# GpSimd's table units of the last stage in one go: from four gated places to slot 34

## The chip, the cores and the metric

The kernel runs on one core of one Trainium2 chip. A core has five engines with a queue of instructions each: TensorE (PE: matrix products; its weight loads are listed as PEld), VectorE (DVE), ScalarE (ACT), GpSimd (POOL) and SyncE (SP), and 16 DMA engines that they share. Each engine works through its own queue in order and waits on semaphores for the others. The metric is the time of one execution on the device in microseconds, as the median of several runs. The profile is one more execution, recorded by the hardware profiler; its times count from the first instruction. "L410" is line 410 of the kernel's file.

## The reference

Eight sequences of 3008 tokens with 256 channels are filtered by a Fourier transform along the sequence, a product with a complex filter and the transform back. Each token then goes through a feed-forward layer of 2048 hidden units with an exact GELU:

```python
X = np.fft.rfft(x, axis=1)
y = np.fft.irfft(X * (filt_r + 1j * filt_i)[None], n=x.shape[1], axis=1)
h = y.reshape(24064, 256) @ w_in
g = 0.5 * h * (1.0 + erf(h / sqrt(2)))
out = g @ w_out
```

## The kernel before, in words

**Stages.** The transform of length 3008 = 47 x 64 is done by matrix products with tables of sines and cosines. Batch 0 has a path of its own at the start (`c1` to `c4`). For each of the batches 1 to 7 there are four stages: `fold` and `s1` (over the 47), `s2` (over the 64) with the filter, `s3` (back over the 64) and `s4` (back over the 47). Between the stages the data are turned by writing them to DRAM and reading them back on SP's queue (`R1`, read by `r1` into `b_sb`; `R2`, read by `r2` into `d_sb`). `s4` writes its result into a ring `y_sb` of two batches.

**The feed-forward layer** goes over tiles of 512 tokens, 47 of them. `mm1` makes one of 16 blocks of hidden units: two products into a `ps_h` bank of PSUM (there are three), and GELU by ACT (L643) into `g_sb`. The second product follows a tile later. For tiles 0 to 2 it is plain (`mm2_first`; VectorE copies the result to `ost` at L660). From tile 3 on, `mm2_seven` does it in seven half-size products m = 0 to 6 in the manner of Strassen and Winograd. VectorE makes their sums of inputs (`sums_1` L685, `sums_2` L691, `sums_3` L696) and puts the results together (L729 to L743) from two `ps_o` banks: m = 0 goes to one, m = 1 and 2 to the other, m = 3 and 4 to the first again, m = 5 and 6 to the second again. The product m = 2 reads what L691 makes, m = 6 what L696 makes. `ost`, `t_sb` and the two results of a tile share a pool of four output buffers. Most output rows are stored by DMAs that GpSimd issues (L761), a few by SP.

**Order of the work.** It is written by hand: the program's main loop has 16 slots per tile, each with one `mm1` and a sixteenth of the second product, and `put(slot, function, arguments)` hangs everything else on a slot; what hangs on a slot is issued before the slot's products. Each engine gets its instructions in the order in which the loop issues them. In the trace slot 27 begins at 58.6 us, slot 33 at 63.4, slot 49 at 78.7 and slot 64 at 93.6; a slot lasts 0.75 to 0.87 us. For batch 1, `s2` stands at slots 27, 41 and 54, `s3` at 38, 52 and 66. `s2_out` (L467) multiplies the result of `s2`, in PSUM, with the filter `Fu`, in SBUF; `s2_sum` (L473, L474) adds and subtracts halves of these products; `s3` needs these sums, first those of one part, in its second half those of the other.

**The filter.** It is loaded into a tile `F` and moved by 36 DMAs of SP into the order `Fu` (`move_filters`, L130; the last 20 at slot 18). The space of `F` is then used again: one piece for `s4_sb`, the sums that L696 makes, two for `v_sb`, and one, `T4a`, for the table of `s4`.

**The table of `s4`.** `table_4_rows` and `weights_4` (slot 9, GpSimd) prepare rows and weights. `table_4_factors` turns them by three small products (L391) and three evacuations by ACT into the factors `G` and `fcs`. `table_4_all` makes the table out of the factors in eight units, each for eight of 32 columns and one of two halves: two products (L410) into a scratch tile `tmp_sb` and their sum (L412) into `T4a`. The scratch tile comes from the pool of `d_sb`, of three buffers. The first `s4` of batch 1 runs on TensorE at 107.4 us. In the kernel before, the factors stand at slot 49, and the units go by twos, at slots 67, 87, 98 and 105, each call with a scratch tile of its own. Ahead of those at 67, 87 and 98 stands a gate: `gate` copies one element of a tile on GpSimd, so that GpSimd's queue waits there until the tile is written.

**GpSimd's queue** also issues the loads of x for the next batch (`load_next`: a gate, then L101), at slots 32, 34, 42, 46, 76, 77, 80 and 81 for batch 2, and the output stores of L761. `fold` (L109, L110) needs these loads.

Of the kernel before, what the change touches and what calls it, by code (L numbers as in the profile page):

```python
# [20 lines left out]
HB = 32  # L21
# [761 lines left out]
def kernel(  # L783
# [9 lines left out]
    m = _Mix(ctx, tc, x, filt_r, filt_i, moe_w_in, moe_w_out, out)  # L793
# [4 lines left out]
    g = m.small  # L798
# [113 lines left out]
    def put(slot, f, *a):  # L912
        at.setdefault(slot, []).append((f, a))
# [5 lines left out]
    for b in range(1, B):  # L919
# [5 lines left out]
        for c in range(4):  # L925
            slot = (4, 8, 11, 13)[c] if b == 1 else s1 + int(c * n1)
# [46 lines left out]
    put(9, m.table_4_rows, g)  # L973
    put(9, m.weights_4, g)
    put(23, m.table_u)
    put(49, m.table_4_factors, g)
    for t, slot in ((3, 67), (5, 98)):
        put(slot, lambda t=t: m.gate(m.st["s", t][0:1, 7, 1, 255:256]))
    put(87, lambda: m.gate(m.st["x1"][0:1, 1, 11, 0:1]))
    parts = [(w, h) for w in range(0, HB, 8) for h in range(2)]  # L980
    for i, slot in enumerate((67, 87, 98, 105)):
        put(slot, m.table_4_all, parts[2 * i:2 * i + 2])
    put(18, m.move_filters, 2, 4)
    put(20, m.weight_sums)
    plain = (0, 1, 2)
# [9 lines left out]
    for s in range((NT + 1) * 16):  # L995
        t, jc = s // 16, s % 16
# [44 lines left out]
```

## Time and profile before

| what | us |
|---|---|
| median of 3 runs (733.98 to 734.56) | 734.04 |
| span of the profiled execution, first to last instruction | 732.0 |
| TensorE busy, share of the span | 713.6, 97% |
| VectorE busy | 597.0, 82% |
| ScalarE busy | 576.5, 79% |
| GpSimd busy | 286.2, 39% |

The profiled execution's own time is its span of 732.0 us and what lies around it; the runs' median is 2.0 us more than the span. The TensorE clock was granted in full (0.999). The page gives each engine's busy time, and for each wait what ended it; a wait of an engine that is not the bound costs nothing by itself. In a timeline the columns are the start, the time (with several instructions in one row: from the first start to the last end), engine, line, operation, what is written from what, shapes and the number of instructions; in brackets stands the idle time ahead and what ended it. In the list of waits the columns after the colon are the sum, the number of waits and the longest.

GpSimd's time around the table:

| stretch, us | GpSimd |
|---|---|
| 63.8 to 67.8 | gates and x loads of slots 32 and 34 |
| 70.9 to 79.1 | stores, gates and x loads of slots 42 and 46 |
| 87.4 to 96.3 | two groups of three stores |
| 96.4 to 103.4 | table units 1 and 2 |
| 104.3 to 115.1 | gates, x loads of slots 76 to 81, stores |
| 115.3 to 120.7 | table units 3 and 4 |
| 127.8 to 140.8 | table units 5 to 8 |

### The profile page before, as it was taken

The page shows a single profiled execution, that of the slowest core. Times are in us where ns is not written, and L with a number is a line of the kernel's source. Part 1 is how long each engine was busy: PE and PEld are TensorE (multiplying, and loading weights), DVE is VectorE, ACT ScalarE, POOL GpSimd, SP SyncE. Part 2 cuts the span into 40 slices and gives each one's busy share as a digit, 9 for nine tenths or more (in the row PEclk, how much of TensorE's full clock was granted, in tenths as well). Part 3 has the DMA queues.
Part 4 walks back from the last instruction along what each step waited for, and adds up shares of the span by engine and source line. Part 5 has one row for each costly group of instructions (what it writes and reads, how often), then busy time and mean ns, then how long its engine had stood idle before and what let it go on. Part 6 is the DMA issues. An engine that isn't in the chain of part 4 may idle for free.

```text
span 732.0 us, 22073 instructions
## 1 busy us (share of the span) xinstructions
PE 713.6 (97%) x9016; PEld 505.9 (69%) x9165; DVE 597.0 (82%) x1091; ACT 576.5 (79%) x1050; POOL 286.2 (39%) x546
## 2 busy tenths in 40 slices
PE   7999999999999999999999999999999999999997
PEld 4846675676777666666677667666677767777776
DVE  8975698899878998798976999779988897775666
ACT  7997778688877888778887788877888788877773
POOL 7853377864223452135511364115531121121121
PEclk9999999999999999999999999999999999999999
DMA  9886544765355553646535455355545442411011
GB/s 158 160 173 161 155 89 123 201 124 100 88 169 143 120 112 107 178 99 134 128 107 162 114 132 119 97 149 151 110 102 135 141 117 84 114 47 42 30 59 59
DMA packets 81254, 87.72 MB, mean 120 GB/s; under 512 B 13393, under 2 KB 61137, under 8 KB 81153
## 3 DMA queue, kind: packets, MB, share of 16 engines
q0 software_dynamic: 22288, 39.50, 24.3%
q1 hardware_dynamic: 58449, 46.62, 23.8%
q8 instruction: 71, 1.16, 0.7%
q14 instruction: 30, 0.25, 0.1%
q10 hardware_dynamic: 416, 0.20, 0.1%
HBM read 54.00 MB, written 46.66 MB: 138 GB/s over the span
## 4 chain that ended last, share of the span: by engine, by line
PE 86%; DVE 4%; DMA 4%; issue 2%; POOL 2%; ACT 1%; DVEq 0%; POOLq 0%; ACTq 0%
PE ps_o L714 38%; PE ps_h L640 38%; PE ps_s L514 3%; PE ps_o L656 2%; PE ps_s L429 2%; PE ps_s L487 2%; DMA x_sb<-in_x_dram 2%; PE ps_s L456 2%; DVE s_sb L685 1%; DMA w_out_sb<-in_moe_w_out_dram 1%; POOL F L137 1%; DMA F<-in_filt_i_dram 1%; ACT g_sb L643 1%; DVE p L467 1%; POOL x_sb L92 1%
## 5 line engine op out<-in xcount | busy, mean ns | idle before, releaser
L643 ACT ACTIVATE g_sb<-ps_h 128x512 f16<-128x512 f32 x752 | 446.4, 601 | 139.9 <-PE ps_h L640 115.5
L640 PE MATMUL ps_h<-y_sb,w_in_sb 128*128 128x512 bf16 (+3 forms) x1455 | 415.0, 365 | 1.5 <-DVE p L467 0.7
L761 POOL DMA_DIRECT2D out_dram<-ost x231 | 131.4, 575 | 388.0 <-DVE ost L743 361.3
L714 PEld LDWEIGHTS <-g_sb 128*128 128x128 f16 x2816 | 184.4, 98 | 80.7 <-issue 14.6
L640 PEld LDWEIGHTS <-w_in_sb 128*128 128x128 bf16 x1600 | 126.3, 98 | 8.3 <-issue 2.4
L714 PE MATMUL ps_o<-w_sums,g_sb 128*128 128x128 f16 x1408 | 121.7, 219 | 1.7 <-DVE g_sb L691 0.2
L714 PE MATMUL ps_o<-w_sums,s_sb 128*128 128x128 f16 x1408 | 121.2, 219 | 1.6
L714 PEld LDWEIGHTS <-s_sb 128*128 128x128 f16 x1408 | 95.1, 98 | 37.6 <-issue 2.5
L685 DVE TENSOR_TENSOR s_sb<-g_sb 128x1024 f16<-128x1024 f16 x176 | 116.4, 692 | 0.4 <-ACT g_sb L643 0.3
L714 PE MATMUL ps_o<-w_out_sb,g_sb 128*128 128x128 f16 x1408 | 113.7, 219 | 1.8
L467 DVE TENSOR_TENSOR p<-ps_s,Fu 128x1024 bf16<-128x1024 f32 x84 | 101.5, 1216 | 9.1 <-PE ps_s L456 6.5
L101 POOL DMA_DIRECT2D x_sb<-in_x_dram x156 | 79.4, 515 | 3.1 <-issue 1.6
L691 DVE TENSOR_TENSOR g_sb<-s_sb,g_sb 128x1024 f16<-128x1024 f16 x88 | 60.3, 687 | 1.5
L714 PE MATMUL ps_o<-w_out_sb,F 128*128 128x128 f16 x704 | 60.6, 219 | 0.9
L696 DVE TENSOR_TENSOR F<-g_sb 128x1024 f16<-128x1024 f16 x88 | 61.4, 697 | 0.0
L714 PEld LDWEIGHTS <-F 128*128 128x128 f16 x704 | 47.1, 98 | 14.6 <-issue 0.4
L736 DVE TENSOR_TENSOR t_sb<-t_sb,ps_o 128x256 f32<-128x256 f32 x44 | 18.4, 417 | 39.0 <-PE ps_o L714 38.6
L514 PEld LDWEIGHTS <-d_sb 96*128 96x128 bf16 x448 | 31.4, 97 | 26.8 <-issue 1.3
L325 ACT ACTIVATE F<-ps_s 128x512 bf16<-128x512 f32 x83 | 45.5, 607 | 0.1
L325 ACT ACTIVATE y_sb<-ps_s 128x376 bf16<-128x376 f32 x95 | 45.4, 478 | 0.1
L327 DVE CAST a_sb<-ps_s 128x512 bf16<-128x512 f32 x54 | 34.7, 684 | 12.0 <-PE ps_s L429 11.7
L743 DVE TENSOR_TENSOR ost<-t_sb,ps_o 128x256 f32<-128x256 f32 x86 | 32.1, 414 | 13.7 <-PE ps_o L714 13.7
(160 smaller groups left out, 589.2 us busy)
## 6 DMA issues: line engine op xcount, KB each, us to landing
out_dram<-ost POOLq DMA_DIRECT2D x127, 128.0 KB, 2.9
b_sb<-R SPq DMA_DIRECT2D x21, 512.0 KB, 5.1
R<-F SPq DMA_DIRECT2D x84, 128.0 KB, 2.5
d_sb<-R SPq DMA_DIRECT2D x56, 192.0 KB, 4.3
R<-a_sb SPq DMA_DIRECT2D x108, 96.0 KB, 2.2
x_sb<-in_x_dram POOLq DMA_DIRECT2D x48, 94.0 KB, 2.7
x_sb<-in_x_dram POOLq DMA_DIRECT2D x48, 48.0 KB, 2.8
x_sb<-in_x_dram POOLq DMA_DIRECT2D x12, 188.0 KB, 5.0
```

The costliest lines, as they stand in the source:

```text
L101: self.nc.gpsimd.dma_start(out=xt[64 * v + to:64 * v + to + m, h, 4 * c:4 * c + 4 * n, :], in_=xv[h][at:at + m, w:w + 4 * n, :])
L325: self.nc.scalar.activation(out=out, in_=in_, func=AF.Copy, scale=1.0 if scale is None else scale)
L327: self.nc.vector.tensor_copy(out=out, in_=in_)
L467: v(out=w[:, a], in0=ps.unsqueeze(2).to_broadcast([128, 2, 2, 256]), in1=f.unsqueeze(1).to_broadcast([128, 2, 2, 256]), op=ALU.mult)
L514: nc.tensor.matmul(ps[:, 94 * i:94 * i + 94], lhsT=d[:, (grp % 2) * 4 + i, 128 * half:128 * half + 128], rhs=self.T4a[:, 4 * grp + i, 0:2 ...
L640: nc.tensor.matmul(ps[:, o:o + n], lhsT=w[:, dc], rhs=self.ring[:, dc, off:off + n], start=(dc == 0), stop=(dc == 1))
L643: nc.scalar.activation(out=self.st["g", t][:, jc, :], in_=ps, func=AF.Gelu)
L685: self.nc.vector.tensor_tensor(out=self.st["s", t][:, i:i + 2], in0=a, in1=b, op=ALU.subtract)
L691: self.nc.vector.tensor_tensor(out=a21[:, k], in0=self.st["s", t][:, k, 0], in1=a22[:, k], op=ALU.add)
L696: self.nc.vector.tensor_tensor(out=self.s4_sb[:, k], in0=a12[:, k], in1=s2[:, k], op=ALU.subtract)
L714: nc.tensor.matmul(ps[:, (m + 1) % 2, sub, :], lhsT=a[:, i, 128 * sub:128 * sub + 128], rhs=b[:, i], start=i == 0, stop=i == 7)
L761: eng.dma_start(out=out, in_=tile_[lo - r0:lo - r0 + n])
```

## The change

The factors are made at slot 33 instead of 49. One call at slot 34 makes all eight units, with one scratch tile. The three gates ahead of the units go. On GpSimd's queue the 24 operations of the units now follow the x loads of slot 34, ahead of the stores of tile 1 and the x loads of slots 42 and 46. The other engines' queues keep their order, but for the factors' products and evacuations. The buffers of the output pool are handed out in another order: in the changed program the first `t_sb` (L729) takes the buffer of the first stores of tile 1, and the first result (L731) that of the second.

```diff
-    put(49, m.table_4_factors, g)
-    for t, slot in ((3, 67), (5, 98)):
-        put(slot, lambda t=t: m.gate(m.st["s", t][0:1, 7, 1, 255:256]))
-    put(87, lambda: m.gate(m.st["x1"][0:1, 1, 11, 0:1]))
-    parts = [(w, h) for w in range(0, HB, 8) for h in range(2)]
-    for i, slot in enumerate((67, 87, 98, 105)):
-        put(slot, m.table_4_all, parts[2 * i:2 * i + 2])
+    put(33, m.table_4_factors, g)
+    put(34, m.table_4_all, [(w, h) for w in range(0, HB, 8) for h in range(2)])
```

## Prediction

> **What bounds the kernel now.** I read the busy shares first, then the waits of each engine, then the timeline of GpSimd and VectorE where the tables are made, then TensorE's own timeline there.
>
> ```profile
> span 732.0 us, 22073 instructions
> PE 713.6 (97%) x9016; PEld 505.9 (69%) x9165; DVE 597.0 (82%) x1091; ACT 576.5 (79%) x1050; POOL 286.2 (39%) x546
> ```
>
> TensorE is the bound, so the change is worth only what it takes from, or adds to, TensorE's waits. TensorE's waits between 44 and 150 us, the stretch that holds all the moved work, are three:
>
> ```profile
> PE ps_h L640 <- DVE p L467: 0.7, 1, 0.7
> PE ps_o L656 <- DMA w_out_sb<-in_moe_w_out_dram: 0.3, 1, 0.3
> PE ps_o L714 <- DVE g_sb L691: 0.2, 1, 0.2
> ```
>
> The middle one, at 44.0 us, lies ahead of the change. The others end at 143.22 and 110.22. Counted from start to start, with 0.057 us for a 128-column matmul, TensorE was due at 142.22 + 3 x 0.057 = 142.39 and at 109.62 + 4 x 0.057 = 109.85: it lost 0.83 and 0.37 us. Both waits are for VectorE, and VectorE is late beside GpSimd's table:
>
> ```profile
> 96.44 1.60 POOL L410 TENSOR_TENSOR tmp_sb<-t_sb 96x376 f32<-96x376 f32 x2
> 98.12 1.32 POOL L412 TENSOR_TENSOR F<-tmp_sb 96x376 bf16<-96x376 f32 x1
> ...
> 115.28 1.61 POOL L410 TENSOR_TENSOR tmp_sb<-t_sb 96x376 f32<-96x376 f32 x2
> 116.96 0.98 POOL L412 TENSOR_TENSOR F<-tmp_sb 96x376 bf16<-96x376 f32 x1
> 118.03 1.61 POOL L410 TENSOR_TENSOR tmp_sb<-t_sb 96x376 f32<-96x376 f32 x2
> ```
>
> ```profile
> 96.57 2.02 DVE L696 TENSOR_TENSOR F<-g_sb 128x1024 f16<-128x1024 f16 x1
> 98.52 1.47 DVE L109 TENSOR_TENSOR xs<-x_sb 111x1024 bf16<-111x1024 bf16 x1
> ...
> 116.28 1.29 DVE L327 CAST a_sb<-ps_s 128x512 bf16<-128x512 f32 x2 [1.18 <-PE ps_s L429]
> 117.49 0.41 DVE L736 TENSOR_TENSOR t_sb<-t_sb,ps_o 128x256 f32<-128x256 f32 x1
> ```
>
> VectorE's operations with two SBUF inputs (L696, L109, L110, L685; 0.68 us alone) last 1.2 to 2.0 us beside a table operation: each waits for the one in flight. Those with a PSUM input (L327, L736, L737, L743) keep their 0.69 and 0.41. An undisturbed unit (two L410, one L412) takes 118.03 - 115.28 = 2.75 us.
>
> **What it removes.** The eight units at 96.4-103.4, 115.3-120.7 and 127.8-140.8 leave their places, and the three one-element gates ahead of them go. VectorE gets back 1.34 + 0.79 + 0.50 + 0.79 = 3.4 us at 96-104 (L696, L109, L110, L109 above 0.68) and 0.79 + 0.10 + 0.79 = 1.7 us at 135-141 (three L685). What TensorE gets of it:
> - At 143.22: VectorE ran without a pause from 133.78 to the L467 that frees the `ps_h` bank (141.95 to 143.17). Its L743 at 138.58 waits for matmuls that end near 138.0, so at most 0.5 of the first 0.9 us counts, then the 0.79 of the L685 at 139.84. L467 would end at 143.17 - 0.5 - 0.79 = 141.9, before 142.39. The whole wait goes: **-0.83 us**. What is late next has 0.5 us of room.
> - At 110.22: L691 follows L743, whose matmuls end near 107.2; it started at 107.56. At most 0.3 of 0.37 can come back. I take **-0.2**.
>
> **What it moves forward.** The three small matmuls and three ACT evacuations of the factors stand at slot 33 (63.4 us) instead of 49 (78.7). Their inputs on GpSimd are done at 54.8 and 56.9, their PSUM bank is freed by the second L467 at 61.4. ACT pauses 0.27 us in each 0.87 us slot there as at slot 49 (its 0.83 us is caught up in about three slots, with three `ps_h` banks between): 0.
>
> GpSimd is in order. The x loads of slots 32 and 34 end on it at 67.80; then come the units, ahead of everything else:
> - First two L410: 67.8-69.4. The first L412 writes where filters lie that `move_filters` still reads; it waits for the last of these 36 DMAs (SP issues it at 68.58, it lands at 71.1): 71.2-72.2. Seven units at 2.75: 91.5 us. VectorE's two-input operations add about 0.2 us for each that gets between (five): 92.5. So GpSimd stays busy 20.1 us longer where it now mostly waits.
> - At 78.16-79.5 VectorE makes the four sums L473/L474 (0.41 each, two SBUF inputs), free now. Each will wait for one table operation: with L410 at 0.82, L412 at 0.98 and about 0.3 us for the sum to end after it, they end at 78.9, 79.85, 81.0 and 82.0. TensorE's s3 begins at 81.73 and needs the last two after half its 0.64 us, at about 82.05. A wait of 0 to 3.8 us (the upper end if each sum loses to two operations, as L696 at 96.57 did, 2.02 us long); nearer to one (six of the seven lengthened ones lost to one). I take **+0.4**.
> - L685 at 90.42 and the sum after it meet the last unit: VectorE is 1.4 us later at 94.4 than now (93.04). The s3 at 95.33 still gets its sums, the product m = 2 gets L691 for its second half (98.4) at 97.5 instead of 96.17. 0, with about 0.9 us of room.
> - The output stores of 70.92, the loads of the next batch of 73.47 and 75.44 and the stores of 78.54, 87.41 and 94.54 start behind the table. Issues last 1.85 us for three stores, 1.6 and 2.2 us for gate and loads: stores at 92.6-94.4, loads at 95.0-98.9, the single store at 99.0, the rest until 103.2, in time for the gate of 104.33. In the changed program VectorE's L729 (97.5) takes the output buffer of the first three stores, landed by 97, and its L731 (now 101.14) that of the single store, landed at 99.0 + 2.9 = 101.9 by the median of such stores. L734 behind it then ends at 102.7; the product that reuses its PSUM bank starts at 103.49. The fold at 102.5 needs loads landed at 98.9 + 2.7 = 101.6. 0, with 0.8 us of room.
>
> **Sum.** -0.83 - 0.2 + 0.4 = -0.6 us on an execution whose span is 732.0 us; the median of the runs, 734.04, holds 2.0 us more around the span, and nothing here touches that. Forecast: 734.04 - 0.6 = **733.4 us**. A measurement of this kernel can tell some 0.2% (1.5 us) from no change, so this is "the same".
>
> **A rule weighed.** No row of before has an L467 (PSUM times SBUF, 1.21 us) beside a table operation; seven of them will be. The nearest rows, L736 and L743 with one PSUM input, keep their time: 0; the farthest, L685 in SBUF, loses 0.79 each. I take 0, and 0.79 is priced in rival A. [...]
>
> **Rivals.**
> - A, **slower: GpSimd's late queue reaches VectorE's output buffers.** The point is the end of the table: up to about 93.3 us the single store lands in time, and each us beyond it delays L731 and L734, and with them the product m = 5 that TensorE begins at 103.49, by one. If the seven L467 contend, or the units take as long as the lengthened ones of now (3.08 us, from 96.44 to 99.52, where seven would end at 93.8 and with waits later), the table ends near 97; the wait is 97 - 93.3 = 3.7, the sum -0.83 + 3.7 + 0.4 = +3.3: 737.3; with half that wait 735.5. For it: little room (0.8 us), and stores have taken 4.6 us to land in the dense stretch at 70.9. Against: later ones took 2.0 to 3.5. Chance 0.22.
> - B, **slower: the four sums lose to two table operations each.** They end at 85.8 and s3 waits 3.8 us: -1.0 + 3.8 = +2.8, 736.8. One row of seven is for it. Chance 0.10.
> - C, **nothing gained:** another wait stands right behind both that go, and the sums cost 0.4: 734.4. TensorE's list shows none, but it names the last releaser only. Chance 0.06.
> - D, **faster:** more of VectorE's 3.4 + 1.7 = 5.1 us reaches TensorE than the two waits show: if a third of it does and the sums cost nothing, -1.7, 732.3. The list of waits speaks against it, and so does VectorE's idle time behind the first part (1.2 us at 111.7). Chance 0.12.
> - That the change doesn't take effect: the programs differ as said, and the units have no wait but the 71.1 us; nothing is kept for it.
>
> The forecast has 0.50. Faster by over 0.2%: D, 0.12. Within: forecast and C, 0.56. Slower: A and B, 0.32. The range leaves out the far half of A and most of D: 732.4 to 737.0; the forecast's own is 732.8 to 735.0.
>
> **What would show it.** Right: table operations without a pause from 71.2 to 92-93 us and none after; L473/L474 at 78 of up to 1.2 us; all L685, L696 and L109 after 95 at 0.68; no wait at 143; a wait of some tenths at s3 near 82. Wrong: L467 longer than 1.25 us beside the table, a table that ends after 94, VectorE idle ahead of L729 or L731 on a store, TensorE waiting near 103.5 for L734, or a wait at 143 that stays.

## The result, and the profile after

The changed kernel takes 739.07 us (median of 6 runs, 736.88 to 741.05), the kernel before 734.26 us (733.98 to 734.57, 6 runs beside them). The ratio is 1.0067, 95% interval 1.0055 to 1.0079: slower by 0.67%, above the predicted range. The profiled execution took 740.88 us. First its head on the page of the changed kernel, with the line of the granted clock in 40 slices of the span:

```profile
span 737.4 us, 22068 instructions
PE 717.5 (97%) x9016; PEld 507.3 (69%) x9165; DVE 594.8 (81%) x1091; ACT 576.7 (78%) x1050; POOL 282.2 (38%) x543
...
PEclk9999989999999999999999999999999999999999
```

VectorE and GpSimd are busy for less time than before (594.8 against 597.0, 282.2 against 286.2), as the change wants it, and the span is 5.4 us longer. One slice shows a lower TensorE clock. TensorE's waits between 44 and 150 us, the same stretch as in the prediction:

```profile
PE ps_s L487 <- DVE p L473: 2.4, 2, 1.9
PE ps_o L714 <- DVE ost L660: 0.4, 1, 0.4
PE ps_o L714 <- issue: 0.2, 1, 0.2
PE ps_o L714 <- DVE g_sb L691: 0.2, 1, 0.2
```

The wait at 143 us (L640, 0.7) is gone, as forecast. New are two waits of `s3` (L487) for VectorE's sums, one of a product for `ost`, and a short one behind them. The timeline of TensorE places them:

```profile
97.66 0.78 PE L487 MATMUL ps_s<-p,U 32*64 32x256 bf16 x16 [1.93 <-DVE p L473]
...
98.93 0.77 PE L487 MATMUL ps_s<-p,U 32*64 32x256 bf16 x16 [0.50 <-DVE p L473]
...
100.47 0.69 PE L714 MATMUL ps_o<-w_out_sb,g_sb 128*128 128x128 f16 x5 [0.44 <-DVE ost L660]
```

This is the `s3` of slot 66, which the prediction had at 95.33 and safe. In the kernel before it ran in one piece, without a wait:

```profile
95.33 0.64 PE L487 MATMUL ps_s<-p,U 32*64 32x256 bf16 x32
```

VectorE was late there in the changed kernel; its timeline ahead of it shows why:

```profile
87.36 1.21 DVE L467 TENSOR_TENSOR p<-ps_s,Fu 128x1024 bf16<-128x1024 f32 x1
...
94.32 2.36 DVE L467 TENSOR_TENSOR p<-ps_s,Fu 128x1024 bf16<-128x1024 f32 x2 [5.75 <-POOL gate L142]
```

Between two instructions of one kind, the four L467 of slot 54, VectorE stands still for 5.75 us, and what it waits for is not data but `gate`, on GpSimd. Before, the second to the fourth of these four followed each other:

```profile
87.03 3.47 DVE L467 TENSOR_TENSOR p<-ps_s,Fu 128x1024 bf16<-128x1024 f32 x3
```

GpSimd's timeline at the end of the table:

```profile
91.33 0.98 POOL L412 TENSOR_TENSOR F<-tmp_sb 96x376 bf16<-96x376 f32 x1
92.25 1.86 POOL L761 DMA_DIRECT2D out_dram<-ost  x3
94.10 0.18 POOL L142 COPY gate<-p 1x1 bf16<-1x1 bf16 x1
94.23 1.11 POOL L101 DMA_DIRECT2D x_sb<-in_x_dram  x2
```

The table ends at 92.31 (92.5 was predicted). The gate at 94.10 is that of the x loads of slot 42. Before, it ran at 72.95:

```profile
72.95 0.18 POOL L142 COPY gate<-p 1x1 bf16<-1x1 bf16 x1 [0.18 <-DVE p L467]
```

**The theory that follows.** `s2_out` makes its output tiles `p` in a pool of three buffers (`self.pp`, L46). The third L467 of slot 54 begins a new tile, and the buffer that comes round is that of tile `p` number 2 of the same batch. `s3` of slot 52 was done with that tile at about 83 us; its last reader is now the gate of slot 42, which copies one element of it on GpSimd (`load_next`, L149). The gate is meant to hold back the loads until that tile is written. But as a reader it also holds the tile's buffer until it has run, and it stands in GpSimd's queue behind the table and three stores. The wait of L467 for that gate is in the program before too; there the gate was done at 73.13 us, 15 us before that L467 began.

To see what this did to the end, I compared the start of the same matmuls in both traces, each from its own span's start. TensorE of the changed kernel lags by 0.23 us ahead of the `s3` of slot 52, by 0.31 to 0.33 from there to slot 65, by 6.47 at slot 69, and by 5.68 from slot 116 on, where the wait at 143 no longer stands; the span is 5.4 longer. From slot 65 to slot 69 the lag grows by 6.1 us, yet the waits in the list come to only 3.0 us without that for L691, which was there before. The rest falls into a stretch in which the clock was low. In the windows of one and two us (the columns are the stretch; its length; busy time of PE, PEld, DVE, ACT and POOL with the number of instructions; the granted clock; the DMA share and GB/s):

```profile
96.00:97.00 1.00, 0.00 (x0) 0.00 (x0) 1.00 (x2) 0.37 (x1) 1.00 (x3) 1.00 0.96 152
97.00:98.00 1.00, 0.32 (x10) 0.14 (x10) 1.00 (x4) 0.00 (x0) 1.00 (x3) 0.94 0.65 96
98.00:99.00 1.00, 0.50 (x16) 0.21 (x16) 1.00 (x3) 0.00 (x0) 1.00 (x2) 0.50 0.76 178
...
103.00:104.00 1.00, 1.00 (x8) 0.72 (x7) 0.96 (x3) 0.98 (x3) 0.00 (x0) 0.50 0.75 228
104.00:106.00 2.00, 2.00 (x21) 1.36 (x19) 0.61 (x1) 0.96 (x3) 0.00 (x0) 0.83 0.59 138
```

TensorE is idle for the whole us from 96, and from 97.87 its clock is granted at 0.50 for 6.83 us. So the loss has two parts, the wait and the slow clock behind it. The rivals to this theory: the table itself slows VectorE (the sums at 78 us, and L467 beside the table, rivals A and B of the prediction); the late stores hold the output buffers (rival A); or the late x loads, not the gate ahead of them, cost the time.

### The profile page after: what moved, and what is told of

Read it like the earlier page. It is cut to its first block, busy times and chain, and to the rows that moved or that the text cites. A ratio compares the mean times of both kernels' runs of the same rounds, so it can differ in the third digit from the quotient of the medians.

```text
span 737.4 us, 22068 instructions
## 1 busy us (share of the span) xinstructions
PE 717.5 (97%) x9016; PEld 507.3 (69%) x9165; DVE 594.8 (81%) x1091; ACT 576.7 (78%) x1050; POOL 282.2 (38%) x543
## 4 chain that ended last, share of the span: by engine, by line
PE 84%; POOL 4%; DMA 4%; issue 3%; ACT 3%; DVE 1%; SPq 1%; POOLq 0%; DVEq 0%; ACTq 0%
PE ps_o L714 38%; PE ps_h L640 36%; PE ps_s L514 3%; PE ps_s L429 2%; POOL tmp_sb L410 2%; PE ps_s L456 1%; PE ps_s L487 1%; ACT g_sb L643 1%; SPq L130 1%; POOL F L412 1%; DMA x_sb<-in_x_dram 1%; ACT y_sb L325 1%; DMA b_sb<-R 1%; DMA F<-in_filt_i_dram 1%; PE ps_c L587 1%
## 5 line engine op out<-in xcount | busy, mean ns | idle before, releaser
L640 PE MATMUL ps_h<-y_sb,w_in_sb 128*128 128x512 bf16 (+3 forms) x1455 | 416.2, 366 | 0.8 <-ACT g_sb L643 0.3
L640 PEld LDWEIGHTS <-w_in_sb 128*128 128x128 bf16 x1600 | 126.5, 98 | 7.6 <-issue 1.6
L685 DVE TENSOR_TENSOR s_sb<-g_sb 128x1024 f16<-128x1024 f16 x176 | 114.9, 684 | 0.7 <-ACT g_sb L643 0.6
L467 DVE TENSOR_TENSOR p<-ps_s,Fu 128x1024 bf16<-128x1024 f32 x84 | 101.8, 1219 | 14.8 <-PE ps_s L456 7.5
L691 DVE TENSOR_TENSOR g_sb<-s_sb,g_sb 128x1024 f16<-128x1024 f16 x88 | 60.4, 688 | 1.5
L514 PEld LDWEIGHTS <-d_sb 96*128 96x128 bf16 x448 | 31.4, 97 | 26.8 <-issue 1.3
L743 DVE TENSOR_TENSOR ost<-t_sb,ps_o 128x256 f32<-128x256 f32 x86 | 32.2, 416 | 14.1 <-PE ps_o L714 14.1
```

Of the source, the lines that this page charges most:

```text
L467: v(out=w[:, a], in0=ps.unsqueeze(2).to_broadcast([128, 2, 2, 256]), in1=f.unsqueeze(1).to_broadcast([128, 2, 2, 256]), op=ALU.mult)
L514: nc.tensor.matmul(ps[:, 94 * i:94 * i + 94], lhsT=d[:, (grp % 2) * 4 + i, 128 * half:128 * half + 128], rhs=self.T4a[:, 4 * grp + i, 0:2 ...
L640: nc.tensor.matmul(ps[:, o:o + n], lhsT=w[:, dc], rhs=self.ring[:, dc, off:off + n], start=(dc == 0), stop=(dc == 1))
L685: self.nc.vector.tensor_tensor(out=self.st["s", t][:, i:i + 2], in0=a, in1=b, op=ALU.subtract)
L691: self.nc.vector.tensor_tensor(out=a21[:, k], in0=self.st["s", t][:, k, 0], in1=a22[:, k], op=ALU.add)
```

## The experiments

All were timed beside the kernel before (medians 734.12 and 734.21 us, 27 runs each). `filler` and `late_gate` do extra work whose result is not used; no kernel leaves out any of the computation.

**1. The changed kernel without the two gates.** The six x loads of slots 42 and 46 stay where they are in the queue, and only the two reads of `p` go.

```diff
             self.gate(self.st[b, "d", 0][0:1, 0, 0:1])
-        else:
+        elif b > 1 or c == 0:
             self.gate(self.st[b, "p", p][0:1, p % 2, 1, 0, 0:1])
```

> The changed kernel without the two gates (slots 42 and 46) whose x loads stand behind the table. Theory H (held tile): in the changed kernel the third L467 of slot 54 waits 5.7 us because the tile p that it takes over is still to be read by the gate of slot 42, which stands behind the table on GpSimd. Without that gate the L467 follows at 88.6 us, TensorE's wait at the s3 of slot 66 goes, the clock stays at 1.00, and the time is 0.8 us under before: 733.4. Rival T (the table itself: the lock between GpSimd and VectorE and the late stores): the table stands as before, so the time stays near 739. Rival X (late x loads): loads still come behind the table, 739.

Measured: 733.24 us (732.63 to 734.31, 11 runs), ratio 0.9988 (0.9979 to 0.9996). TensorE's waits between 44 and 150 us:

```profile
PE ps_s L487 <- DVE p L474: 0.4, 1, 0.4
PE ps_o L714 <- DVE g_sb L691: 0.2, 1, 0.2
PE ps_o L656 <- DMA w_out_sb<-in_moe_w_out_dram: 0.2, 1, 0.2
```

Table, late loads and late stores are all still there, and the whole loss is gone with two copies of one element. What stays is the wait at `s3` near 82 us that the prediction had priced at 0.4.

**2. The changed kernel with a fourth buffer for `p`.** Gates and table stay; L467 takes another buffer.

```diff
-        self.pp = pool("pp", 3)
+        self.pp = pool("pp", 4)
```

> The changed kernel with a fourth buffer for the tiles p; all gates stay. H: the third L467 takes a tile that was last read by the gate of slot 34, long done; no wait at 88.6, time 733.4, as without the gates. If the gate mattered through the loads behind it and not through the tile that it reads: no change, 739.

Measured: 732.87 us (732.72 to 734.33, 11 runs), ratio 0.9989 (0.9981 to 0.9998). Its GpSimd and VectorE timelines:

```profile
94.87 0.73 POOL L142 COPY gate<-p 1x1 bf16<-1x1 bf16 x1
```

```profile
87.78 3.47 DVE L467 TENSOR_TENSOR p<-ps_s,Fu 128x1024 bf16<-128x1024 f32 x3
```

The gate is as late as in the changed kernel, at 94.87, and L467 no longer waits for it: three of them run on, as in the kernel before. So it is the buffer that the gate holds, not the gate's time on GpSimd.

**3. Six units at slot 34, two at 87.** The six units end at 86.4 us, ahead of the point where L467 wants the buffer.

```diff
-    put(34, m.table_4_all, [(w, h) for w in range(0, HB, 8) for h in range(2)])
+    parts = [(w, h) for w in range(0, HB, 8) for h in range(2)]
+    put(34, m.table_4_all, parts[:6])
+    put(87, m.table_4_all, parts[6:])
```

> The changed kernel with six units at slot 34 and two at slot 87. The gate of slot 42 comes at 94.1 - 2 x 2.75 = 88.6 us, when the third L467 would start anyway (88.6). H: a wait of 0 to 0.3 us at that L467, none at s3, time 733.4. T: three quarters of the table stand where they stood, so three quarters of the loss stay: 738.

Measured: 733.47 us (732.52 to 733.93, 11 runs), ratio 0.999 (0.9981 to 0.9998). The gate ran at 88.24; L467 waited 0.3 us for it, which reached TensorE nowhere.

**4. Useless products ahead of `s3` of slot 66**, to separate the wait from the slow clock behind it: TensorE has eight products of 512 columns to do while VectorE is late.

```diff
+    def fill(self, n):
+        ps = self.bank("ps_fill", "f")
+        for i in range(n):
+            self.nc.tensor.matmul(ps, lhsT=self.ones[:, 0:128], rhs=self.ones, start=True, stop=True)
...
+    at.setdefault(66, []).insert(0, (m.fill, (8,)))
```

> The changed kernel with eight products of 512 columns (1.7 us, results unused) on TensorE ahead of the s3 of slot 66, inside its wait of 2.0 us. Theory C (clock): some 2.6 us of the loss are the wait for VectorE less the 0.8 us won at 143, and the rest, which differs from run to run with the mean granted clock (736.9 us at 1.000, 741 at 0.995), is TensorE at half clock after it stood still. With the filler the clock stays at 1.00 and the time is 736 to 738 in all runs, though TensorE does 1.7 us more. If the low clock has another cause: 739 in the median and the same spread of 4 us.

Measured: 737.97 us (736.78 to 739.37, 5 runs), ratio 1.005 (1.0036 to 1.0063); two of the five runs lie above what was expected. In its trace the eight products fill the gap, and the clock stays whole (timeline, then windows with the columns as above; L492 is this kernel's L487):

```profile
95.43 1.89 PE L325 MATMUL ps_fill<-ones 128*128 128x512 bf16 x8
...
97.52 0.65 PE L492 MATMUL ps_s<-p,U 32*64 32x256 bf16 x16 [0.20 <-DVE p L478]
```

```profile
96.00:97.00 1.00, 1.00 (x7) 0.39 (x4) 1.00 (x2) 0.23 (x1) 1.00 (x3) 1.00 0.97 148
...
98.00:99.00 1.00, 0.38 (x16) 0.12 (x8) 1.00 (x4) 0.00 (x0) 1.00 (x2) 1.00 0.75 176
...
103.00:104.00 1.00, 1.00 (x15) 0.76 (x13) 0.96 (x3) 1.00 (x3) 0.00 (x0) 1.00 0.71 230
```

With the full clock the lag to the kernel before grows from 0.19 to 4.29 us over slots 64 to 66, against 6.1 in the changed kernel: by this comparison 4.1 is the wait and 2.0 the clock. (The list of the changed kernel shows 3.0 of waits, since a TensorE at half clock comes later to the next wait: the waits at 98.93 and 100.47 are 0.50 and 0.44 there, their like in `filler`, at full clock, 0.62 and 0.67.)

The times support this only in part, for the intervals of the two ratios overlap. The profiled execution of `filler` also lost 0.27 us at 196 and 1.20 at 551, where `s4` (L514) started late, the second time waiting for `d_sb` from DRAM; the traces of the kernel before and of the changed kernel have no such loss, and without it the 738.54 us of this execution would be 737.1. The six runs of the changed kernel spread by 4 us, and their times go with the mean granted clock: 736.88 us at 1.000, 737.50 and 738.81 at 0.998, 739.32 at 0.997, 740.88 and 741.05 at 0.995. (Of the 740.88 us of the profiled execution 3.5 lie around its span, against 1.8 to 2.9 in the others; the spans, from 734.9 to 738.2, spread by 3.3.) The run at 1.000 should be the wait alone: 736.88 - 734.26 = 2.6, which with the 0.83 gained at 143 makes a wait of 3.4, not far from 4.1. Half clock for 6.83 of 737 us takes 0.5 x 6.83 / 737 = 0.0046 from the mean, so 0.995 is one such fall. What the clock did in the runs at 0.997 and 0.998 isn't known, nor in the one run of `filler` (739.37 us) that has 0.998 too; only the profiled executions show it over time.

**5. The kernel before with the gate made late.** The table stays in its four places; 79 `iota` instructions stand ahead of the gate of slot 42 on GpSimd, and so ahead of the loads and stores behind it too.

```diff
+    put(41, lambda: [nc.gpsimd.iota(m.cols, pattern=[[1, 128]], base=0, channel_multiplier=0,
+                                    allow_small_or_imprecise_dtypes=True) for i in range(79)])
```

> The kernel before, its table where it was, with 79 small iotas (0.27 us each, some 21 us, into a tile that nothing reads any more) on GpSimd ahead of the gate of slot 42, which so comes near 94 us as in the changed kernel. [...] H: the third L467 of slot 54 waits some 5.5 us for the gate, TensorE waits at the s3 of slot 66, and the loss is that of the changed kernel and the 0.8 us at 143 that are not won here: 737.7 at full clock, up to 742. T: no table stands at 68 to 92, so 734.1.

Measured: 742.73 us (742.33 to 743.39, 4 runs), ratio 1.0116 (1.0101 to 1.0132), 0.7 above the upper end of what was expected. From start to start one `iota` took 0.306 us there, more than I had put, so the gate ran at 96.93, not at 94. GpSimd and VectorE:

```profile
96.93 0.18 POOL L142 COPY gate<-p 1x1 bf16<-1x1 bf16 x1
```

```profile
97.14 2.35 DVE L467 TENSOR_TENSOR p<-ps_s,Fu 128x1024 bf16<-128x1024 f32 x2 [8.88 <-POOL gate L142]
```

And TensorE's waits from 44 to 150 us:

```profile
PE ps_s L487 <- DVE p L473: 5.6, 2, 5.1
PE ps_h L640 <- DVE p L467: 0.7, 1, 0.7
```

The loss stands at the same place, without any of the change's own instructions, and is larger, as the gate comes 2.8 us later than in the changed kernel. That the loads and stores behind the gate are late too is unlikely to matter: here they began at 97.26 and 100.42, in experiment 1 at 95.25 and 98.29, and there nothing was lost. Beside the `iota` instructions VectorE's L467 at 84.71 and 87.05 took 1.22 and 1.21 us, as alone. The clock falls here too, to 0.50 for 6.83 us from 100.77, and all four runs have a mean of 0.995. The wait at 143 stays, since the table still runs there.

**6. Seven units at slot 34, one at 87**, as experiment 3 with 7 in place of 6: a dose between.

> Seven units at slot 34 and one at slot 87. The gate comes at 91.4 us, the third L467 is 2.8 us late instead of 5.7. H, with the room that TensorE has there (the sums behind would end 2.7 us earlier than in the changed kernel, at 96.5, where s3 needs them at 96.3): a wait of 0.2 to 1.0 us, time 733.5 to 734.3, so half the delay costs far less than half of the loss. If the loss went with the delay one to one: 736.

Measured: 734.74 us (733.99 to 735.71, 11 runs), ratio 1.0007 (0.9998 to 1.0015), some 0.4 above what was expected. VectorE's and TensorE's waits:

```profile
DVE p L467 <- POOL gate L142: 2.1, 1, 2.1
```

```profile
PE ps_o L714 <- DVE ost L660: 0.3, 1, 0.3
PE ps_o L714 <- DVE g_sb L691: 0.2, 1, 0.2
```

The gate ran at 90.59. Of the 2.1 us VectorE had most as room; TensorE lost 0.46, for `ost` at 96.95. So the loss sets in between gates at 88.24 and 90.59. In four traces the wait of L467 is the gate's end, 0.18 after its start, less 88.2 to 88.7, when it was due:

| kernel | gate of slot 42 at | L467 waits | TensorE later near slot 66 |
|---|---|---|---|
| `units_6_2` | 88.24 | 0.3 | none seen |
| `units_7_1` | 90.59 | 2.1 | 0.46 |
| the changed kernel | 94.10 | 5.75 | 6.1, of it 2.0 clock |
| `late_gate` | 96.93 | 8.88 | lag of 9.35 at the end |

**7. Control: the kernel before without the two gates.** The edit is that of experiment 1.

> Control: the kernel before without the gates of slots 42 and 46. H: the gate is read long before the tile is taken over (73 against 88 us), so nothing changes: 734.1. If taking these gates away were worth something by itself (earlier loads, less on GpSimd), it would be under 733.6, and the gain of the same edit on the changed kernel would be no evidence for H.

Measured: 733.61 us (733.21 to 734.72, 11 runs), ratio 0.9992 (0.9983 to 1.0001). That is 0.6 below the median beside it, but the interval includes 1, and in its trace TensorE has the waits of before (0.7 for L640 at 143, 0.2 for L691) and no lag to it from slot 10 to the end. I can't tell a gain of the gates themselves from none; if it were real, some of the gain in experiment 1 would be this. Experiments 2, 3 and 8 keep both gates and gain as much, so the gain there doesn't come from the gates.

**8. The kernel before with only its last four units moved.** Units 5 to 8 go to slot 34, the factors to 33; the first four stay at 67 and 87.

```diff
-    put(49, m.table_4_factors, g)
-    for t, slot in ((3, 67), (5, 98)):
-        put(slot, lambda t=t: m.gate(m.st["s", t][0:1, 7, 1, 255:256]))
+    put(33, m.table_4_factors, g)
+    put(67, lambda t=3: m.gate(m.st["s", t][0:1, 7, 1, 255:256]))
...
-    for i, slot in enumerate((67, 87, 98, 105)):
+    put(34, m.table_4_all, parts[4:])
+    for i, slot in enumerate((67, 87)):
         put(slot, m.table_4_all, parts[2 * i:2 * i + 2])
```

> The kernel before with the four units of slots 98 and 105 alone moved to slot 34 (factors at 33, the gate of slot 98 gone); the units of 67 and 87 and their gates stay. The gate of slot 42 comes near 83 us, before its tile is wanted. The part of the prediction on 143 us: without table operations at 128 to 141 the wait of 0.83 us there goes, 733.3. If that wait had another cause, 734.1.

Measured: 733.08 us (732.67 to 733.96, 11 runs), ratio 0.9986 (0.9978 to 0.9995). The wait at 143 is gone and nothing new stands on TensorE between 44 and 150: its list has the waits for `w_out_sb` (0.4) and for L691 (0.2) alone, both of which were there before.

With `no_gate_c1`, `four_p` and `units_6_2` this is one of four versions that beat both kernels, if by little: 0.10% to 0.14% below the kernel before, all four intervals below 1, and not told apart from each other.

## Why the prediction was wrong

**The step that failed** is the one on stores and loads behind the table: "Issues last 1.85 us for three stores, 1.6 and 2.2 us for gate and loads". It counted the gates as issue time on GpSimd's queue, and asked who waits for the stores and for the loads. It did not ask who waits for what a gate *reads*. The price of that step was put at 0, with 0.8 us of room; it was 6.1 us on TensorE in the profiled execution. None of the rivals had this mechanism. Rival A was of the same kind, a buffer given back late by GpSimd's queue, but looked at the output pool, and its 3.3 us came from a table that ends near 97; the table ended at 92.31.

The row that would have told it was in the trace of before. The gate at 72.95 waits for an L467: so it reads a tile that L467 writes, and whoever writes that buffer next waits for the gate. With three buffers and one tile for each pair of L467, the next writer comes three tiles later, the third L467 of slot 54, at about 88.2 (87.03 and one L467). Against a table that was to end at 92.5 with 1.85 for three stores behind it, the gate ends at 94.5 and makes it some 6 us late.

**The slow clock** was not in the prediction either: about 2.0 of the 6.1 us in the profiled execution.

**What held and what did not**, term by term:
- The wait at 143.22 (-0.83): gone in the changed kernel and in every experiment without units at 128 to 141 us; it stays where they stay (`late_gate`, `before_no_gate_c1`).
- The wait at 110.22 (-0.2): wrong by its whole size. It stayed at 0.37 in every kernel. L691 runs when L743's matmuls let it; what VectorE got back ahead of that was no use.
- The four sums at 78 (+0.4): counted from start to start, TensorE lost 0.08 us in the changed kernel, 0.6, 0.33 and 0.12 in `no_gate_c1`, `four_p` and `units_6_2`. No sum lost to two table operations, as rival B had it; VectorE's timeline of the changed kernel:

```profile
78.77 0.52 DVE L473 TENSOR_TENSOR p<-p 128x512 bf16<-128x512 bf16 x1
79.21 1.04 DVE L474 TENSOR_TENSOR p<-p 128x512 bf16<-128x512 bf16 x1
80.18 1.20 DVE L473 TENSOR_TENSOR p<-p 128x512 bf16<-128x512 bf16 x1
81.30 1.04 DVE L474 TENSOR_TENSOR p<-p 128x512 bf16<-128x512 bf16 x1
```

- L467 beside the table (0, against 0.79 each): six of them, the one at 87.36 above included, ran beside it and took 1.21 to 1.23 us; alone, in the kernel before, they take the same 1.21 to 1.23. So the 0, which the prediction took from the nearest rows, was right.
- The table's timeline: first L412 at 71.65 (71.2 predicted), last one ended at 92.31 (92.5). The 20.1 us by which GpSimd was to stay busy longer isn't worked out in the prediction, and nothing in its sum uses it.
- The output buffers (0, with 0.8 us of room): in `four_p`, where L467 is not late, VectorE's L731 waited 2.9 us for a store, and TensorE lost about 0.5 us at 109.7 and 110.9. In `no_gate_c1` it waited 1.1, and in the changed kernel 1.6 (put down to another DMA), and TensorE lost nothing there. So rival A's mechanism is there, with at most 0.5 of its 3.7 us; that the 0.5 us come from this wait was not tested. The wait in VectorE's list of `four_p`:

```profile
DVE ost L731 <- DMA out_dram<-ost: 2.9, 1, 2.9
```

With the one missing step taken out, the sum comes close: 733.4 was forecast, `no_gate_c1` and `four_p` took 733.24 and 732.87. Part of that is luck. From slot 49 to behind 143 us, TensorE gained only 0.2 us in the trace of `no_gate_c1` (0.83 less the 0.6 at the four sums) and nothing in that of `four_p` (0.83 less 0.33 and 0.5), while the medians fell by 0.9 and 1.25. Each trace is one execution, slower than its median (734.16 and 733.55 us), and where the rest of the gain comes from wasn't found.

## What to carry to other kernels

An instruction on an in-order queue that only reads a tile, even one element of it, keeps that tile's buffer until it has run: the gate at 94.10, a copy of 0.18 us, held L467 for 5.75 us, and with a fourth buffer the gate at 94.87 did not hold it. When long work is put ahead of a queue, list for every instruction behind it not only who needs its result, but also who writes next into what it reads; the pool's number of buffers tells how soon. And a gap of 1.9 us on TensorE, as in the changed kernel, can cost twice: once as the wait and once more as a slow clock behind it (4.1 and 2.0 us in the profiled execution, by the comparison with `filler`), so the price of a late input is not the wait alone.

## What the runs showed of the hardware that was not expected

TensorE's granted clock fell to 0.50 after idle stretches of 1.9 us (the changed kernel, from 97.87) and of 5.1 us (`late_gate`, from 100.77), both times for 6.83 us, and in the first case not in every run: six runs had mean clocks from 0.995 to 1.000. With products in the gap it stayed at 1.00 (the trace of `filler`). In the profiled execution of the changed kernel the clock fell 0.2 us behind the idle stretch of 1.9 us, ahead of the second wait at `s3`, which began at 98.43. What decides whether a gap slows the clock, and why the fall lasts 6.83 us, no run here tests.

VectorE's sums with two inputs in SBUF, 0.41 us alone, took 0.52 to 1.20 us beside GpSimd's table, and its product with one input in PSUM kept its 1.21 to 1.23 (the traces of the kernel before and of the changed kernel).
